# Window attention and two MLPs: scores of the float32 items folded to 128 columns, and a planner that knows when v lands

## The chip, the cores and the metric

One core of one Trainium2 chip. The metric is device time in microseconds of one execution, lower is better. PE is TensorE, DVE VectorE, ACT ScalarE, POOL GpSimd, SP the engine whose queue issues the loads.

## The reference

```python
# attention: B, H, S, D = 4, 8, 576, 64; window 128
scores = q @ k.T / sqrt(D) - slope[h] * abs(i - j)      # where 0 <= i - j < 128, else -1e9
attn = exp(scores - max(scores)); attn = attn / (sum(attn) + 1e-9)
x = (attn @ v)                                          # as 2304 x 512
# first MLP: 512 -> 2048 -> 512
h = x @ w_in; g = max(h, 0) + alpha * min(h, 0); x = g @ w_out
# second MLP: 512 -> 2048 -> 512
h = x @ w2_in; g = h / (1 + exp(-1.702 * h)); out = g @ w2_out
```

All inputs and the output are float32. Slopes are 2^-(h+1).

## The kernel before

The attention is cut into 64 items, one for each batch, head and unit. Unit 0 holds the queries 0 to 255 (32 items), unit 1 the rest. The first 24 items (`FP = 24`), all of unit 0, are computed in float32 at the start of the kernel and are called the float32 items; the other 40 are split into high and low parts and run later, beside the first MLP. Items are numbered n; two neighbouring items are two heads.

A unit 0 item has two chunks of 128 queries. The first attends to 128 keys, the second to 256: the 128 keys before it (of which a query sees those of an upper triangle) and its own 128 (a lower triangle). For each query exactly one of the two keys in the same column of these halves is inside the window. Steps of a float32 item, with the name that the planner gives them:

- raw: q, k and v are loaded by SP in two DMAs (L516 to L520), into five buffers in turn.
- s: scores on PE, one matmul a chunk, 128 and 256 columns (L568).
- bias: on DVE, scores plus bias with a running minimum, one custom instruction a chunk (L596), with a small instruction that reads the minimum out. The bias table relht has 256 columns a head, in bfloat16; outside the window it holds a large negative number.
- exp on ACT, an instruction a chunk (L612); add on POOL, sum plus 1e-9 (L627); recip (L622) and norm (L643, two scalings) on DVE.
- tr: on PE, transposes of 128 x 128 by an identity matrix, one for the first chunk and two for the second (L658); pt: ACT copies the 384 columns out of PSUM (L665).
- vz: POOL copies v beside zeros (L554), so that two heads share one output; x: on PE, attention times v (L715), two matmuls of 256 and 128 columns.
- xh on ACT and xl on DVE split the output of a pair of heads (L200, L205) for the MLP, which multiplies in three passes (high by high, high by low, low by high).

Weights of the first MLP come as 64-bit words and are decoded in 32 chunks: ld (SP), sc1 and sc2 (ACT, L245, L251), sh and ad (DVE, L255, L260), hi (ACT, L200), lo (DVE, L205). These are steps of the planner as well. The first MLP has steps h (L786, 12 matmuls), n (L800, ACT), g (L806, DVE), gh (ACT), gl (DVE) and o (L836, 12 matmuls). Step i of h needs weight chunk 2 * (i // 2), and g of step i - 2.

What sets the order: `emission()` runs a list planner over all these steps. PE's order is written out by hand: in each round scores of item n + 1, warm-up matmuls (`WARM`, only in the first seven rounds), v of item n - XLAG, transposes of item n - 1; after the rounds the h and o steps. The other engines take, among steps whose needs are met, the one that can start first and then the one with the earliest due time, worked out from a cost for each step (`COST`) and a delay for each engine (`DELAY`). `FIRST` gives the times at which the first five loads of q and k land; v is taken to be there with them. The list is issued in the order of planned start times, and `chain` fixes that order on each engine. Before the list stand memsets, the loads of the first five items and of the bias table (in four DMAs, for heads 0, 1, 2 to 3 and 4 to 7), and nine warm-up matmuls.

After the float32 items come 32 planned steps of the first MLP with the weight decoding beside them, from step 28 on with the split items; then the rest of the first MLP and the second, in an order of their own that the diff does not touch.

Of the kernel before, what the change touches and what calls it, by code (L numbers as in the profile page):

```python
# [39 lines left out]
PTF = {0: (0, 256, 0), 1: (256, 192, 128)}  # L40
# [28 lines left out]
EXTRA = {("g", SPLIT): 1.5}  # L69
# [4 lines left out]
def emission():  # L74
# [10 lines left out]
    for i in range(FP):  # L85
        ops |= {(k, i) for k in ("bias", "exp", "add", "recip", "norm", "vz", "pt")}
        ops |= {(k, i) for k in ("xh", "xl")[: 2 * (i % 2)]} | {("raw", i)}
# [4 lines left out]
    def needs(k, i):  # L92
        if k in ("s", "tr"):
# [3 lines left out]
            x=(("pt", i), ("vz", i), ("xl", i - 3)),  # L97
# [10 lines left out]
    deps = {z: [y for y in needs(*z) if y in ops] for z in ops}  # L108
    after = {z: [] for z in ops}
    for z in ops:  # L110
        for y in deps[z]:
            after[y].append((z, DELAY[COST[y[0]][0]] if COST[y[0]][0] != COST[z[0]][0] else 0))
# [18 lines left out]
    free, end, out = dict.fromkeys(ENGINES, 0.0), {}, []  # L131
# [3 lines left out]
    while any(wait.values()):  # L135
        best = None
        for e, l in wait.items():
            for z in l[: 1 if e == "PE" else 40]:
                if all(y in end for y in deps[z]):
                    t = max([free[e]] + [end[y] + (DELAY[COST[y[0]][0]] if COST[y[0]][0] != e else 0) for y in deps[z]])  # L140
# [22 lines left out]
def tile_window_attention__then__two_mlps(  # L163
# [265 lines left out]
    vzf = [first.tile([P, 2, P], F32, name=f"vzf{i}") for i in range(2)]  # L429
# [14 lines left out]
    def make_own():  # L444
        for t, n, below in ((own, P, False), (own2, D, True)):
            nc.gpsimd.memset(t, 1.0)
            nc.gpsimd.affine_select(
                out=t, in_=t, pattern=[[1 if below else -1, n]], compare_op=ALU.is_ge,
                fill=0.0, base=0, channel_multiplier=-1 if below else 1,
            )  # L450
# [97 lines left out]
    def a_split_v(n, b, u, h, U):  # L548
# [3 lines left out]
        if n < FP:  # L552
            d0 = (h % 2) * D
            nc.gpsimd.tensor_copy(vzs[n % 4][:, :, d0 : d0 + D], vr)  # L554
            return
# [5 lines left out]
    def a_qk(n, b, u, h, U):  # L561
        s = bank_of("s").rearrange("p (c k) -> p c k", k=256)
        places = []
        for i, (c0, rows, kk, keys) in enumerate(U["chunks"]):
            o = s[:rows, i, :]
            if n < FP:
# [4 lines left out]
                places.append(o[:, :keys])  # L571
# [7 lines left out]
        st["s", n] = places if n < FP else s  # L579

    @stage
    def a_bias(n, b, u, h, U):
        tt, s = work_of(n)
        places = st.pop(("s", n))
        m = len(U["chunks"])
        if n >= FP:
            x, places = places, []
            i0 = 1 - u
            nc.vector.copy_predicated(
                x[:, i0:m, :P], own.bitcast(U32).unsqueeze(1).to_broadcast([P, m - i0, P]), x[:, i0:m, P:]  # L590
            )
        for i, (c0, rows, kk, keys) in enumerate(U["chunks"]):
            off = kk - (c0 - P)
            if n >= FP:
                off = P if u == 0 and i == 0 else 0
            nc.vector.tensor_tensor_reduce(  # L596
                out=tt[:rows, i * 256 : i * 256 + keys] if n < FP else tt[:, i * P : (i + 1) * P],
                in0=places[i] if n < FP else x[:, i, :P],
                in1=relht[:rows, h, off : off + keys] if n < FP else relt[:, off : off + P],
# [4 lines left out]
                accum_out=s[:rows, i : i + 1],  # L604
# [3 lines left out]
    def a_exp(n, b, u, h, U):  # L608
        tt, s = work_of(n)
        for i, (c0, rows, kk, keys) in enumerate(U["chunks"]):  # L610
            t = tt[:rows, i * 256 : i * 256 + keys] if n < FP else tt[:, i * P : (i + 1) * P]
            nc.scalar.activation(  # L612
                t, t, AF.Exp, bias=s[:rows, i : i + 1], scale=-1.0, accum_out=s[:rows, 4 + i : 5 + i]
            )
# [14 lines left out]
    @stage  # L629
    def a_norm(n, b, u, h, U, eng):  # L630
        tt, s = work_of(n)
        if n >= FP:
            m = len(U["chunks"])
            t = tt[:, : m * P].rearrange("p (c k) -> p c k", k=P)
            nc.vector.tensor_tensor(t, t, s[:, 12 : 12 + m].unsqueeze(2).to_broadcast([P, m, P]), op=ALU.mult)
            return
        for i, (c0, rows, kk, keys) in enumerate(U["chunks"]):
            t = tt[:rows, i * 256 : i * 256 + keys]
            r = s[:rows, 12 + i : 13 + i]
            if eng == "act" or (eng == "mix" and i):  # L640
                nc.scalar.mul(t, t, r)
            else:
                nc.vector.tensor_scalar(t, t, r, None, op0=ALU.mult)  # L643

    @stage
    def a_trans(n, b, u, h, U):
        tt = work_of(n)[0]
        x = bank_of("pt")
        for i, (c0, rows, kk, keys) in enumerate(U["chunks"]):
            if n >= FP:  # L650
                keep(nc.tensor.transpose(x[:, i * P : (i + 1) * P], tt[:, i * P : (i + 1) * P], ident))  # L651
                continue
            for j in range(kk // P, (kk + keys) // P):
                col, nq, oc = PTF[j]
                dst = col + (c0 - U["q0"] - oc)

                src = tt[:, i * 256 + j * P - kk : i * 256 + j * P - kk + P]
                nc.tensor.transpose(x[:, dst : dst + P], src, ident)  # L658
# [3 lines left out]
    def a_pt_hi(n, b, u, h, U):  # L662
        x = st["t", n]
        if n < FP:
            nc.scalar.copy(pts[n % 3], x[:, :384])  # L665
        else:
            nc.scalar.copy(ar["th"][:, : U["nq"]], x[:, : U["nq"]])

# [36 lines left out]
    def a_av(n, b, u, h, U):  # L705
        if n < FP:
# [6 lines left out]
            pt, vz = pts[n % 3], vzs[n % 4]  # L713
# [459 lines left out]
    for t in vzs:  # L1173
        nc.gpsimd.memset(t, 0.0)
    for t in sts:
        nc.gpsimd.memset(t, 1.0)
# [6 lines left out]
    bias_load(0, 1)  # L1183
# [3 lines left out]
    bias_load(1, 1)  # L1187
    a_load(1, (1,))
    a_load(3, (0,))
    bias_load(2, 2)  # L1190
# [3 lines left out]
    bias_load(4, 4)  # L1194
    a_load(4, (1,))
    make_identity(nc, ident)
    make_own()
# [18 lines left out]
    def piece(name, fn):  # L1216
# [8 lines left out]
        norm=lambda n: a_norm(n, "dve"), vz=a_split_v, pt=a_pt_hi, xh=lambda n: a_xf(n, 0), xl=lambda n: a_xf(n, 1),  # L1225
        raw=a_load, ld=piece("load", w_load), sc1=w_scale_hi, sc2=piece("scale", w_scale_lo), sh=piece("shift", w_shift),
# [25 lines left out]
    def item_b(n):  # L1252
        o = n - 1 if n > FP else -1
        return (
            lambda: (n == FP + 2 and item_t(o), a_recip(n), a_split_v(n), a_load(n + 2), a_norm(n, "dve")),
# [18 lines left out]
    for k, i in emission():  # L1274
        if (k, i) == ("n", 0):
            joint()
        if k == "n" and i % 2:
# [277 lines left out]
```

## Time and profile before

| | us |
|---|---|
| median of the three runs shown | 873.68 |
| the runs | 873.65, 873.68, 881.98 |
| the profiled execution, its own time | 872.37 |
| its span, first to last instruction | 870.5 |
| PE busy in it | 862.5 (99%) |
| DVE, ACT, POOL busy | 695.5, 550.3, 186.1 |

The profile is of one execution. Times in a timeline are microseconds from the first instruction. A PE instruction counts as busy from its issue to a modelled end, so that a PE that is busy by the rows may still have waited; the distance from start to start tells it. The same distance is what an instruction costs on the other engines, since the end of one overlaps the beginning of the next.

### The profile page before, as it was taken

What the parts mean: (1) busy time and instruction counts of PE and PEld (TensorE: products, weight loads), DVE (VectorE), ACT (ScalarE), POOL (GpSimd) and SP (SyncE); (2) the same over time, 40 slices, a digit from 0 to 9 for tenths busy, and PEclk for the clock granted to TensorE, in tenths of its full rate; (3) what the DMA queues carried; (4) which work ended last, traced back from release to release, by engine and by line L of the source; (5) the groups of instructions that cost most, each with busy time, mean ns of one, the idle gap of its engine ahead of it and who ended that gap; (6) DMA issues with size and microseconds to landing.
All of it is one profiled execution on the core that took longest, in us unless ns stands there. A gap on an engine that the chain in (4) does not pass through costs nothing.

```text
span 870.5 us, 19438 instructions
## 1 busy us (share of the span) xinstructions
PE 862.5 (99%) x6804; PEld 835.7 (96%) x6804; DVE 695.5 (80%) x1763; ACT 550.3 (63%) x1397; POOL 186.1 (21%) x351
## 2 busy tenths in 40 slices
PE   9999999999999999999999999999999999999998
PEld 7899999999999999999988889999999999999998
DVE  6899886789899999998477777547474799988875
ACT  6999877677766776766355558656556764444433
POOL 4300003456656656655000000000000000000000
PEclk9999999999999999999999999999999999999999
DMA  5857742235244343351043344766678873634423
GB/s 156 218 158 230 249 138 95 78 98 178 78 125 152 91 127 115 90 172 29 25 146 98 98 142 147 235 222 230 233 250 293 286 249 112 178 125 134 146 61 98
DMA packets 74210, 132.29 MB, mean 152 GB/s; under 512 B 14336, under 2 KB 33792, under 8 KB 74112
## 3 DMA queue, kind: packets, MB, share of 16 engines
q1 hardware_dynamic: 74112, 131.05, 47.4%
q8 instruction: 54, 0.88, 0.4%
q14 instruction: 44, 0.36, 0.1%
HBM read 94.31 MB, written 36.70 MB: 151 GB/s over the span
## 4 chain that ended last, share of the span: by engine, by line
PE 61%; ACT 0%; DVE 0%; issue 0%; DVEq 0%; ACTq 0%
PE p L1092 19%; PE p L995 15%; PE h L786 9%; PE h L995 6%; PE p L836 5%; PE o L836 4%; PE x L727 1%; PE s L577 1%; PE pt L651 0%; PE s L578 0%; ACT oh L200 0%; DVE ob L1109 0%; ACT G L1004 0%; DVE se L1109 0%; DVE wd L1109 0%
## 5 line engine op out<-in xcount | busy, mean ns | idle before, releaser
L786 PE MATMUL h<-xh,wh 128*128 128x256 f32 (+1 forms) x512 | 149.2, 291 | 0.1
L786 PE MATMUL h<-xh,wl 128*128 128x256 f32 (+1 forms) x512 | 149.0, 291 | 0.0
L786 PE MATMUL h<-xl,wh 128*128 128x256 f32 (+1 forms) x512 | 149.0, 291 | 0.0
L1092 PE MATMUL p<-wl,oh 128*128 128x256 f32 x504 | 136.2, 276 | 0.0
L1092 PE MATMUL p<-wh,oh 128*128 128x256 f32 x504 | 135.0, 277 | 0.3 <-ACT oh L200 0.3
L1092 PE MATMUL p<-wh,ol 128*128 128x256 f32 x504 | 131.1, 276 | 0.0
L836 PE MATMUL o<-gh,wh 128*128 128x256 f32 x448 | 127.6, 285 | 0.0
L836 PE MATMUL o<-gl,wh 128*128 128x256 f32 x448 | 124.1, 277 | 0.8 <-DVE gl L205 0.8
L836 PE MATMUL o<-gh,wl 128*128 128x256 f32 x448 | 123.8, 276 | 0.0
L786 PEld LDWEIGHTS h<-xh,wh 128*128 128x128 f32 x512 | 96.1, 188 | 3.1 <-DVE g L806 0.3
L786 PEld LDWEIGHTS h<-xh,wl 128*128 128x128 f32 x512 | 96.1, 188 | 2.9
L786 PEld LDWEIGHTS h<-xl,wh 128*128 128x128 f32 x512 | 96.1, 188 | 2.7
L1123 POOL TENSOR_TENSOR ob<-wd,se 128x256 f32<-128x256 f32 x1 | 0.7, 746 | 448.2 <-ACT se L1121 448.2
L1092 PEld LDWEIGHTS p<-wl,oh 128*128 128x128 f32 x504 | 94.6, 188 | 0.0
L1092 PEld LDWEIGHTS p<-wh,oh 128*128 128x128 f32 x504 | 93.7, 188 | 0.5 <-ACT oh L200 0.5
L1092 PEld LDWEIGHTS p<-wh,ol 128*128 128x128 f32 x504 | 91.4, 188 | 0.0
L836 PEld LDWEIGHTS o<-gl,wh 128*128 128x128 f32 x448 | 84.3, 188 | 1.1 <-DVE gl L205 1.0
L836 PEld LDWEIGHTS o<-gh,wh 128*128 128x128 f32 x448 | 84.2, 188 | 0.1
L836 PEld LDWEIGHTS o<-gh,wl 128*128 128x128 f32 x448 | 84.1, 188 | 0.0
L800 ACT ACTIVATE n<-h 128x256 f32<-128x256 f32 (+1 forms) x128 | 52.2, 408 | 50.5 <-PE h L786 50.0
L812 ACT CAST gh<-g 128x256 fp32r<-128x256 f32 x112 | 45.3, 404 | 56.3 <-DVE g L806 56.2
L200 ACT CAST oh<-gs 128x1024 fp32r<-128x1024 f32 (+1 forms) x40 | 38.1, 964 | 62.9 <-issue 28.2
(190 smaller groups left out, 2459.2 us busy)
## 6 DMA issues: line engine op xcount, KB each, us to landing
g2d<-G SPq DMA_DIRECT2D x64, 288.0 KB, 3.5
ws<-in_w_in_dram SPq DMA_DIRECT2D x32, 512.0 KB, 3.8
ws<-in_w_out_dram SPq DMA_DIRECT2D x32, 512.0 KB, 4.4
gr<-g2d SPq DMA_DIRECT2D x32, 512.0 KB, 4.3
raw<-in_u_dram SPq DMA_DIRECT2D x32, 352.0 KB, 3.0
raw<-in_u_dram SPq DMA_DIRECT2D x32, 160.0 KB, 2.5
xr<-x2d SPq DMA_DIRECT2D x40, 128.0 KB, 2.6
wo2d<-wd SPq DMA_DIRECT2D x16, 256.0 KB, 2.6
```

The source lines that it names most:

```text
L200: return nc.scalar.copy(o, i)
L577: keep(nc.tensor.matmul(o[:, :n_], q, kh[:, ks : ks + n_], start=True, stop=False))
L727: keep(nc.tensor.matmul(x[:, oc : oc + nq], v, p[:, col : col + nq], start=(i == 0 and k == 0), stop=(i == len(js) - 1 and k == (j < 4)), ...
L786: keep(nc.tensor.matmul(ph, w[:, 0, c * P : (c + 1) * P], x[:, c, r : r + n], start=(c == 0 and i == 0), stop=(c == NC - 1 and i == 2),))
L800: nc.scalar.activation(n, ph, AF.Relu, scale=-1.0)
L812: nc.scalar.copy(gh, g)
L836: keep(nc.tensor.matmul(o, w[:, 1, c * P : (c + 1) * P], g, start=(first and (k == KM or c % 2 == 0) and i == 0), stop=(last and i == 2), ...
L995: tc.keep_in_program_order(nc.tensor.matmul(o, w[:, cc * P : (cc + 1) * P], x[:, h, cc, i, :], start=first and cc == 0 and k == 0, stop=la ...
L1092: mm = nc.tensor.matmul(o[:, m, :], g[:, a, m * P : (m + 1) * P], w, start=(p == 0 and m == 0 and i == 0), stop=(p == NF // 2 - 1 and i == 2),
L1123: nc.gpsimd.tensor_tensor(c11, p1_, p2_, op=ALU.add)
```

## The change

The float32 items are brought to the form of the later items of unit 0. DVE copies the own half of the second chunk's scores over the other half where a triangular mask `own` is set, then adds the bias on 128 columns for both chunks. For this the bias table is folded once: for each group of heads the larger of its two halves is kept, right before the bias of its first item (`HEADS`). Exponentials, scaling (now one instruction with the reciprocals spread over 128 columns each) and transposes (now two) work on 2 x 128 columns. After ACT's copy of 256 columns POOL separates the two triangles of the second chunk (own, then prev, in place); v's matmuls are as before.

The planner: new steps own and prev, new costs, v a known time for the first five items (`FIRST_V`), v matmuls a round later (`XLAG = 4`), six vz buffers instead of four, loads of weights due one round earlier and half a microsecond later in landing (`LATE`). A decoding step that it would place gives way to another step of that engine that is due sooner and can start before the decoding step would be nearly done (`DECODE`).

The start: masks are built before the identity matrix, some memsets go from POOL to DVE, and a small exponential is issued before the list.

```diff
-XLAG = 3
+XLAG = 4
+HEADS = {0: 1, 1: 1, 2: 2, 4: 4}
 ENGINES = dict(
-    PE=dict(s=0.66, tr=0.33, x=0.65, b=0.22, h=1.37, o=1.37),
-    DVE=dict(bias=0.6, recip=0.22, norm=0.5, xl=0.37, sh=0.4, ad=0.63, lo=0.63, g=0.42, gl=0.38),
-    ACT=dict(exp=0.98, pt=0.42, xh=0.31, sc1=0.6, sc2=0.6, hi=0.55, n=0.36, gh=0.34),
-    POOL=dict(vz=0.33, add=0.24),
+    PE=dict(s=0.66, tr=0.22, x=0.65, b=0.22, h=1.37, o=1.37),
+    DVE=dict(bias=0.78, recip=0.22, norm=0.37, xl=0.37, sh=0.4, ad=0.63, lo=0.63, g=0.42, gl=0.38),
+    ACT=dict(exp=0.81, pt=0.29, xh=0.31, sc1=0.6, sc2=0.6, hi=0.55, n=0.36, gh=0.34),
+    POOL=dict(vz=0.33, add=0.24, own=0.31, prev=0.31),
     SP=dict(raw=0.85, ld=2.3),
 )
-COST = {k: (e, c) for e, d in ENGINES.items() for k, c in d.items()}
+COST = {"v": ("SP", 0.0)} | {k: (e, c) for e, d in ENGINES.items() for k, c in d.items()}
+LATE = dict(ld=0.5)
+DECODE = ("sc1", "sc2", "sh", "ad", "hi", "lo")
+FIRST_V = (0.6, 1.8, 4.0, 5.2, 7.6)
-EXTRA = {("g", SPLIT): 1.5}
+EXTRA = {("g", SPLIT): 1.5} | {("bias", i): 0.14 * m for i, m in HEADS.items()}
...
-            x=(("pt", i), ("vz", i), ("xl", i - 3)),
+            x=(("prev", i), ("vz", i), ("xl", i - 3)), own=(("pt", i), ("x", i - 3)), prev=(("own", i),),
-            norm=(("recip", i),), pt=(("tr", i), ("x", i - 3)), vz=(("raw", i), ("x", i - 4)),
+            norm=(("recip", i),), pt=(("tr", i), ("x", i - 3)), vz=(("raw", i), ("v", i), ("x", i - 6)),
-            ld=(("ad", i - NST), ("s", 8 + 2 * i)), sc1=(("ld", i), ("lo", i - NWD)), sc2=(("ld", i),), sh=(("sc1", i),),
+            ld=(("ad", i - NST), ("s", 6 + 2 * i)), sc1=(("ld", i), ("lo", i - NWD)), sc2=(("ld", i),), sh=(("sc1", i),),
...
+        if z[0] in DECODE:
+            near = [(max([free[e]] + [end[y] + lag(y, x) for y in deps[x]]), x) for x in wait[e]
+                    if x[0] not in DECODE and due[x] < due[z] and all(y in end for y in deps[x])]
+            t, z = min([x for x in near if x[0] < t + cost(z) - 0.3], default=(t, z))
...
 def a_bias(n, b, u, h, U):
-        if n >= FP:
-            x, places = places, []
-            i0 = 1 - u
-            nc.vector.copy_predicated(
-                x[:, i0:m, :P], own.bitcast(U32).unsqueeze(1).to_broadcast([P, m - i0, P]), x[:, i0:m, P:]
-            )
+        i0 = 1 - u
+        nc.vector.copy_predicated(
+            x[:, i0:m, :P], own.bitcast(U32).unsqueeze(1).to_broadcast([P, m - i0, P]), x[:, i0:m, P:]
+        )
...
 def a_norm(n, b, u, h, U):
-        for i, (c0, rows, kk, keys) in enumerate(U["chunks"]):
-            t = tt[:rows, i * 256 : i * 256 + keys]
...
-                nc.vector.tensor_scalar(t, t, r, None, op0=ALU.mult)
+        t = tt[:, : m * P].rearrange("p (c k) -> p c k", k=P)
+        nc.vector.tensor_tensor(t, t, s[:, 12 : 12 + m].unsqueeze(2).to_broadcast([P, m, P]), op=ALU.mult)
...
 def a_pt_hi(n, b, u, h, U):
-            nc.scalar.copy(pts[n % 3], x[:, :384])
+            nc.scalar.copy(pts[n % 3][:, : 2 * P], x[:, : 2 * P])
...
+    def a_tri(o, t, below):
+        nc.gpsimd.affine_select(
+            out=o, in_=t, pattern=[[1 if below else -1, P]], compare_op=ALU.is_ge if below else ALU.is_gt,
+            fill=0.0, base=0, channel_multiplier=-1 if below else 1,
+        )
...
+    def a_pt_tri(n, b, u, h, U, below):
+        o, t = pts[n % 3][:, (1 + below) * P : (2 + below) * P], pts[n % 3][:, P : 2 * P]
+        a_tri(o, t, below)
...
+    make_own(own, P, False)
-    for t in vzs:
+    for t in vzs[:2]:
         nc.gpsimd.memset(t, 0.0)
+    make_identity(nc, ident)
+    make_own(own2, D, True)
     for t in sts:
-        nc.gpsimd.memset(t, 1.0)
+        nc.vector.memset(t, 1.0)
+    for t in vzs[2:]:
+        nc.vector.memset(t, 0.0)
+    nc.vector.memset(tb[:, :1], 0.0)
...
-    make_identity(nc, ident)
-    make_own()
+    nc.scalar.activation(tb[:, 1:2], tb[:, :1], AF.Exp)
...
     for k, i in emission():
+        if k == "bias" and i in HEADS:
+            t = relht[:, i : i + HEADS[i]]
+            nc.vector.tensor_tensor(t[:, :, :P], t[:, :, :P], t[:, :, P:], op=ALU.max)
```

## Rows read from the trace of the kernel before

**Rows 1.** Busy time of each engine in stretches: microseconds from and to, then each engine

```profile
core 0: us, PE busy (x) PEld busy (x) DVE busy (x) ACT busy (x) POOL busy (x), PEclk, DMA share, GB/s
11.40:44.00 32.60, 32.28 (x211) 29.43 (x210) 27.98 (x146) 29.39 (x109) 10.72 (x38) 1.00 0.74 197
44.00:52.10 8.10, 7.55 (x54) 6.70 (x52) 7.04 (x22) 7.67 (x21) 1.70 (x12) 1.00 0.31 92
52.10:80.00 27.90, 27.90 (x246) 27.90 (x247) 27.21 (x59) 27.06 (x59) 0.00 (x0) 1.00 0.66 211
...
5.60:52.10 46.50, 45.63 (x296) 40.17 (x294) 39.46 (x191) 41.40 (x145) 13.99 (x56) 1.00 0.66 178
```

**Rows 2.** Timeline of PE, one round of the float32 items: start, duration, instruction

```profile
18.51 0.49 PE L658 MATMUL pt<-ident,tt 128*128 128x128 f32 x3
18.83 0.82 PE L568 MATMUL s<-rawf 128*128 128x128 f32 x4
19.49 0.82 PE L715 MATMUL o<-ptf,vz 128*128 128x256 f32 x4
20.14 0.27 PE L658 MATMUL pt<-ident,tt 128*128 128x128 f32 x1
```

**Rows 3.** Timeline at the handover to the first MLP, PE and DVE

```profile
48.99 0.37 PE L786 MATMUL h<-xh,wh 128*128 128x256 f32 x1
...
50.94 0.69 DVE L205 TENSOR_TENSOR wl<-wd,wh 128x512 fp32r<-128x512 f32 x1 [0.24 <-ACT wh L200]
51.55 0.47 DVE L806 SCALAR_TENSOR_TENSOR g<-n,beta,h 128x256 f32<-128x256 f32 x1
...
52.08 0.38 PE L786 MATMUL h<-xh,wh 128*128 128x256 f32 x1
```

**Rows 4.** Who DVE waits for, 5.60 to 52.10: total, times, longest

```profile
DVE tt L596 <- PE s L568: 4.8, 5, 3.2
DVE st L622 <- POOL st L627: 1.3, 3, 0.5
DVE ttf L596 <- PE s L568: 0.4, 2, 0.2
```

**Rows 5.** Timeline of DVE, an item before, with the xl of a pair

```profile
19.69 0.29 DVE L596 CUSTOM_DVE_ANT_0 tt<-s,relht 128x128 f32<-128x128 f32 x1 [0.21 <-PE s L568]
...
20.25 0.16 DVE L622 RECIPROCAL st<-st 128x2 f32<-128x2 f32 x1
20.52 0.55 DVE L643 TENSOR_SCALAR ttf<-ttf,st 128x128 f32<-128x128 f32 x2
20.99 0.42 DVE L205 TENSOR_TENSOR xl<-o,xh 128x256 fp32r<-128x256 f32 x1
21.33 0.29 DVE L596 CUSTOM_DVE_ANT_0 tt<-s,relht 128x128 f32<-128x128 f32 x1
```

**Rows 6.** Timeline of DVE, item 24, which has the folded form before the change

```profile
125.36 0.29 DVE L589 COPY_PREDICATED s<-own,s 128x128 f32<-128x128 uint32 x1
...
126.11 0.08 DVE L596 DVE_READ_ACCUMULATOR2_ANT st<- 128x1 f32 x1
...
127.14 0.17 DVE L622 RECIPROCAL st<-st 128x2 f32<-128x2 f32 x1
127.34 0.42 DVE L635 TENSOR_TENSOR ts<-ts,st 128x256 f32<-128x256 f32 x1
127.68 0.69 DVE L205 TENSOR_TENSOR gl<-g,gh 128x256 fp32r<-128x256 f32 x1
...
135.88 0.42 DVE L205 TENSOR_TENSOR gl<-g,gh 128x256 fp32r<-128x256 f32 x1
```

**Rows 7.** POOL beside the split items: a timeline row, then groups (busy, mean ns)

```profile
127.48 0.61 POOL L205 TENSOR_TENSOR vp<-raw,vp 128x128 fp32r<-128x128 f32 x1 [0.95 <-ACT vp L557]
...
L676 POOL TENSOR_SCALAR_AFFINE_SELECT ptl<-tl 128x128 fp32r<-128x128 f32 x5 | 2.2, 436 | 1.4 <-DVE st L621 0.7 <-DVE tl L205 0.5
...
L676 POOL TENSOR_SCALAR_AFFINE_SELECT pth<-th 128x128 fp32r<-128x128 f32 x5 | 1.5, 302 | 6.3 <-ACT th L667 6.1
```

More of the change, by code (lines that the diff above doesn't have):

```diff
@@ L85, in emission @@
     for i in range(FP):
-        ops |= {(k, i) for k in ("bias", "exp", "add", "recip", "norm", "vz", "pt")}
+        ops |= {(k, i) for k in ("bias", "exp", "add", "recip", "norm", "vz", "pt", "own", "prev")}
         ops |= {(k, i) for k in ("xh", "xl")[: 2 * (i % 2)]} | {("raw", i)}
@@ L106, in needs, with lag @@
         )[k]
-    deps = {z: [y for y in needs(*z) if y in ops] for z in ops}
-    after = {z: [] for z in ops}
+    def lag(y, z):
+        e = COST[y[0]][0]
+        return DELAY[e] + LATE.get(y[0], 0) if e != COST[z[0]][0] else 0
+    known = {("v", i): t - DELAY["SP"] for i, t in enumerate(FIRST_V)}
+    deps = {z: [y for y in needs(*z) if y in ops or y in known] for z in ops}
+    after = {z: [] for z in (*ops, *known)}
     for z in ops:
         for y in deps[z]:
-            after[y].append((z, DELAY[COST[y[0]][0]] if COST[y[0]][0] != COST[z[0]][0] else 0))
+            after[y].append((z, lag(y, z)))
     for y, z in zip(seq, seq[1:]):
@@ L130, in emission @@
     wait = {e: sorted((z for z in ops if COST[z[0]][0] == e), key=lambda z: (place.get(z, 0), due[z], z)) for e in ENGINES}
-    free, end, out = dict.fromkeys(ENGINES, 0.0), {}, []
+    free, end, out = dict.fromkeys(ENGINES, 0.0), known, []
     for i, t in enumerate(FIRST):
@@ L139, in emission @@
                 if all(y in end for y in deps[z]):
[L140 removed]
+                    t = max([free[e]] + [end[y] + lag(y, z) for y in deps[z]])
                     if best is None or (round(t, 3), due[z], z) < best[0]:
@@ L428, in tile_window_attention__then__two_mlps @@
     rawfs = [first.tile([P, UCOLS[0]], F32, name=f"rawf{i}") for i in range(3)]
-    vzf = [first.tile([P, 2, P], F32, name=f"vzf{i}") for i in range(2)]
+    vzf = [first.tile([P, 2, P], F32, name=f"vzf{i}") for i in range(4)]
     at = ExitStack()
@@ L442, in tile_window_attention__then__two_mlps, with make_own @@
     own2 = ap_.tile([D, D], F32, name="own2")
-    def make_own():
-        for t, n, below in ((own, P, False), (own2, D, True)):
-            nc.gpsimd.memset(t, 1.0)
-            nc.gpsimd.affine_select(
-                out=t, in_=t, pattern=[[1 if below else -1, n]], compare_op=ALU.is_ge,
-                fill=0.0, base=0, channel_multiplier=-1 if below else 1,
-            )
+    def make_own(t, n, below):
+        nc.gpsimd.memset(t, 1.0)
+        nc.gpsimd.affine_select(
+            out=t, in_=t, pattern=[[1 if below else -1, n]], compare_op=ALU.is_ge,
+            fill=0.0, base=0, channel_multiplier=-1 if below else 1,
+        )
     def bank_of(kind):
@@ L603, in a_bias @@
                 op1=ALU.min,
-                accum_out=s[:rows, i : i + 1],
+                accum_out=s[:, i : i + 1],
             )
@@ L609, in a_exp @@
         tt, s = work_of(n)
[L610 to L614, printed above, removed]
+        for i in range(len(U["chunks"])):
+            t = tt[:, i * P : (i + 1) * P]
+            nc.scalar.activation(t, t, AF.Exp, bias=s[:, i : i + 1], scale=-1.0, accum_out=s[:, 4 + i : 5 + i])
     @stage
@@ L629, in a_norm @@
     @stage
-    def a_norm(n, b, u, h, U, eng):
+    def a_norm(n, b, u, h, U):
         tt, s = work_of(n)
[L632 to L637, printed above, removed]
-            t = tt[:rows, i * 256 : i * 256 + keys]
[L639 to L642, printed above, removed]
-                nc.vector.tensor_scalar(t, t, r, None, op0=ALU.mult)
+        m = len(U["chunks"])
+        t = tt[:, : m * P].rearrange("p (c k) -> p c k", k=P)
+        nc.vector.tensor_tensor(t, t, s[:, 12 : 12 + m].unsqueeze(2).to_broadcast([P, m, P]), op=ALU.mult)
     @stage
@@ L648, in a_trans @@
         x = bank_of("pt")
-        for i, (c0, rows, kk, keys) in enumerate(U["chunks"]):
+        for i in range(len(U["chunks"])):
+            t = nc.tensor.transpose(x[:, i * P : (i + 1) * P], tt[:, i * P : (i + 1) * P], ident)
             if n >= FP:
[L651 to L658, printed above, removed]
+                keep(t)
         st["t", n] = x
```

42 lines of the change are left out of this document (20 added, 22 removed).

## The prediction, made before the run

> **What bounds the kernel now.** I read the stretches first (busy time of each engine in five windows), then PE's timeline in the attention stage, then the handover to the first MLP, then who VectorE (DVE) waits for, and last the instructions of one item on DVE before and of one item that already runs in the new form. The granted clock is 1.00 in every stretch [rows 1], so nothing here turns on it. From 52.1 us on PE streams without a break (27.90 of 27.90 us) and its matmuls are not touched by the change; what the change can move is the moment at which that stream starts. So the question is when the third MLP matmul group starts, 52.08 us now.
>
> In the attention stage PE has a fixed round for each of the 24 items: three transposes 0.32 us (18.51 to 18.83), scores 0.66, attention times v 0.65, together 1.63 us [rows 2]. From 18.51 to the first MLP matmul at 48.99 it has 18 transpose groups, 16 of scores and 19 of v to do: 18 x 0.32 + 16 x 0.66 + 19 x 0.65 = 28.7 us in 30.5 us. So PE loses 1.8 us there to waiting, although its busy row shows next to nothing idle. The other engines are as full: in 11.4 to 44.0 us DVE is busy 27.98 and ACT 29.39 of 32.6 us, in 44.0 to 52.1 DVE 7.04 and ACT 7.67 of 8.1 us [rows 1].
>
> At the handover the one that comes last is DVE: the split of the third weight chunk (50.94, 0.69 us), then g of the first group (51.55, 0.47 us, so until 52.02), and 0.06 us later PE starts its third group [rows 3]. Everything DVE must do for the 24 items and for three weight chunks has to lie before that. I therefore add up DVE's time, not PE's.
>
> **The change, part by part.**
>
> *Two transposes instead of three.* A transpose follows the one before it after (0.49 - 0.27) / 2 = 0.11 us [rows 2]. PE's round becomes 1.52 us; over 24 items PE saves 2.6 us. Were PE the bound, this would be a gain in full.
>
> *The same items on DVE.* Before, one item takes 0.56 us from its first bias instruction to the reciprocal (19.69 to 20.25), 0.27 to the scaling, 0.47 for the two scalings, and every second item 0.34 for the low part xl [rows 5]. The new form is in this trace already, at item 24 (same unit, two chunks of 128 columns): copy-predicated and two reductions 125.36 to 126.11 = 0.75 us, reciprocal to scaling 0.20, one scaling over 256 columns 0.34 [rows 6]. So +0.19, -0.07 and -0.13: -0.01 us an item, -0.2 us over 24. DVE gains nothing from the fold; with xl it needs 1.46 us of PE's new 1.52 us round, so that the weight work (about 1.6 us a chunk on DVE) still has no room of its own.
>
> *Folding the bias table.* Four new DVE instructions, over 1, 1, 2 and 4 heads of 128 columns, each right in front of the bias of heads 0, 1, 2 and 4. Nearest rows: a tensor-tensor over 256 columns moves the next instruction by 0.34 us (20.99 to 21.33) [rows 5], one over 512 by 0.61 us (50.94 to 51.55) [rows 3]; by the same slope 0.20 over 128. Sum 0.20 + 0.20 + 0.34 + 0.61 = 1.35 us. The first lies where DVE waits 3.2 us for its first scores [rows 4], the second in the wait for the second scores; 0.95 us stay. They wait for the table's loads too; those of later heads land well before. Bounds: 0 (all in waits of the filling pipeline) to 1.35; I take 0.95.
>
> *What DVE stops waiting for.* From 5.60 to 52.10 us DVE is busy 39.46 of 46.50 us [rows 1]; of the 7.0 us idle, 4.8 + 0.4 - 3.2 = 2.0 us are waits for scores and 1.3 us waits for POOL's sum [rows 4]; the rest is short gaps and weight steps that wait for ACT. With PE's round 0.11 us shorter most waits for scores in the steady part go; in the filling part they stay, since warm-up matmuls set the pace there: 1.2 of 2.0. The scheduler that knows v's landing no longer puts item 1's copy of v ahead of item 0's sum, and one that looks past decoding delays fewer sums: half of the 1.3, 0.65. ACT exponentiates and copies 256 instead of 384 columns an item, so its weight steps come earlier: 0.45. Together 2.3 us, bounds 0 (each gap only moves) to 3.3 + 0.45.
>
> *Edits costed at nothing.* The table load stands at the front already, and ACT is idle until its first exponential; the new dummy one waits for a memset behind seven others on DVE, all in the 3.2 us before the first scores [rows 4]. POOL loses four memsets to DVE there. With v used one round later (XLAG 4, six v buffers) the pipeline drains later: behind the last transposes stand two more selects on POOL of 0.30 to 0.44 us [rows 7], 0.6 to 0.9 us on the last v matmul, and PE's MLP groups queue behind it in program order. PE then comes to its first group that much later after its last transpose, but the third group waits for DVE anyway; if that cover goes, it costs up to 0.9 us. Weight loads are issued one round earlier on SP's queue, between the item loads; DVE's clock is what they feed, and it has no room to use them sooner.
>
> *POOL.* It gets two selects an item: 2 x 0.30 (or 0.44) [rows 7]. It was busy 10.72 of 32.6 us [rows 1]; twenty items add 12.0 to 17.4 us, so it ends at 70% to 86%. It stays under PE's round, so I take no cost, but each sum can now stand behind a select.
>
> *A conflict of two engines.* The low part gl takes 0.69 us where POOL's subtraction of v starts just before it (127.48) and 0.42 us without one (135.88) [rows 6, 7]. The new scaling multiplies two tiles in SBUF, and POOL's new selects read SBUF: each meeting could cost 0.27 us. I take nothing in the sum, since the old scaling and POOL's copies already share these microseconds, and treat it as a rival. The Trainium skill (SBUF — State Buffer, section Who interferes with whom) has this as a rule: a VectorE instruction with two SBUF inputs and a GpSimd instruction that reads SBUF take one port in turns, and whichever starts second waits for the other to finish. By that rule, which the pair of rows bears out, the fold would be paid for on DVE.
>
> **The sum.** 2.3 + 0.2 - 0.95 = 1.5 us earlier start of the stream. The profiled execution took 872.37 us (870.5 span and 1.9 around it) and would take 870.9; the runs shown have their median 1.3 us above that, at 873.68, so the predicted median is 872.2.
>
> **Rivals.**
> 1. *PE is the bound after all.* Then the 2.6 us and the 1.8 us of waiting both go: 4.4 us, 869.3. For it: PE's round is longer than DVE's for an item. Against: DVE's last instruction releases the third group [rows 3], and its total does not fall.
> 2. *Nothing moves.* The gaps on DVE only change place and the table's folding eats what goes: 873.7, within 0.5. For it: the zero bound above, and 3.7 us of DVE's idle time are not waits that the change names.
> 3. *POOL and DVE get in each other's way* (slower). Place: the scaling of each item, and the sum behind POOL's selects. Price 0.27 us for each meeting; it decides from 1.5 / 0.27 = 6 of 24 items on. With 12 of them hit it costs 3.2 us: 873.68 - 1.5 + 3.2 = 875.4. For it: POOL busy over 70%. Against: the order on both engines is fixed and may keep them apart.
> 4. *The fold does not take hold* (the transposes stay at three, or PE's rounds keep 1.63 us): this is case 2 in time.
>
> **How the numbers follow.** Forecast (0.5 to 3 us gained, 870.7 to 873.2) 0.50; rival 1, 0.12; rivals 2 and 4, 0.20; rival 3, 0.18. The range runs from 869.6 (most of rival 1) to 875.6 (most of rival 3); the forecast alone would be 870.7 to 873.2. One per cent, about what a measurement of this kernel can tell from no change, is 8.7 us: twice the whole of rival 1, and four to five times rival 3. So no change within 1% has 0.97, slower 0.02 (for many meetings at POOL along with a late drain), faster 0.01.
>
> **What would show it.** Right: transposes in pairs and rounds near 1.52 us where no weight step stands; the bias of an item 0.75 us and its scaling 0.34 us on DVE; DVE's waits for scores near 0.8 us after the first; the third MLP group at 50.3 to 51.0 us, still released by DVE; everything behind it as before, only earlier. Wrong: the third group before 49.5 us, or released by PE's own last v matmul (rival 1, or a drain that counts); scalings of 0.6 us and more beside POOL's selects, or rounds over 1.63 us (rival 3). A change of more than 1 us between the third group and the end would mean that the order of later work moved too, which I take as unchanged.

## The result, and the profile after

The changed kernel takes 879.39 us (median of 22 runs, 875.96 to 887.2) against 873.66 us before (22 runs, 872.58 to 881.98): ratio 1.0055, 95% interval 1.0039 to 1.0072. It is 5.7 us slower, where 1.5 us less was forecast, and it lies above the range. The profiled execution of after took 887.2 us (span 885.2). From about 710 us on it ran at a pace that the other profiles show only near their end, so behind 140 us I read a second profile of the same kernel (878.2 us span).

First the busy time in the first two stretches of [rows 1], with two stretches more:

```profile
11.40:44.00 32.60, 29.87 (x172) 26.40 (x173) 25.77 (x135) 24.52 (x99) 21.34 (x74) 0.90 0.69 180
44.00:52.10 8.10, 7.45 (x47) 6.47 (x46) 7.37 (x33) 7.07 (x27) 5.98 (x19) 1.00 0.01 4
10.40:14.10 3.70, 0.07 (x1) 0.00 (x1) 0.71 (x3) 0.38 (x2) 1.45 (x6) 0.80 0.51 146
14.10:19.60 5.50, 5.47 (x19) 4.30 (x20) 3.71 (x20) 2.29 (x10) 2.19 (x9) 0.51 0.33 86
```

All engines but POOL are less busy up to 44 us, and PE does 172 instructions instead of 211, partly because it has fewer transposes, partly because it lost time: it stands from 10.40 to 14.10, and then the granted clock is 0.51 (the level of 1.2 GHz) until 19.60. Before, it was 1.00 throughout. The standstill, read from PE, DVE and POOL of after in turn (start, duration, instruction, idle time before it and what ended that):

```profile
14.13 0.66 PE L644 MATMUL pt<-ident,tt 128*128 128x128 f32 x2 [3.66 <-DVE tt L637]
```

```profile
13.28 0.17 DVE L625 RECIPROCAL st<-st 128x2 f32<-128x2 f32 x1 [3.29 <-POOL st L630]
13.55 0.42 DVE L637 TENSOR_TENSOR tt<-tt,st 128x256 f32<-128x256 f32 x1
```

```profile
8.00 0.22 POOL L630 TENSOR_SCALAR st<-st 128x2 f32<-128x2 f32 x1 [1.16 <-ACT tt L617]
12.43 0.29 POOL L565 COPY vzf<-raw 128x128 f32<-128x128 f32 x1 [4.22 <-DMA raw<-in_u_dram]
...
13.04 0.21 POOL L630 TENSOR_SCALAR st<-st 128x2 f32<-128x2 f32 x1
```

PE waits for item 1's scaling, DVE for item 1's sum, and POOL, which makes that sum, for a DMA. What stands in front of the sum is the copy of v of item **5** (12.43), whose loads SP issues at 8.65 and 9.22:

```profile
8.65 0.47 SPq L529 DMA_DIRECT2D raw<-in_u_dram  x1
9.22 0.54 SPq L531 DMA_DIRECT2D raw<-in_u_dram  x1
```

POOL's order in after is: copies of items 0 and 1, sum 0, copies of items 5 and 2, sum 1. Before, the copy of item 5 came behind the sum of item 4.

The waits of [rows 4] are in after, over the same stretch (total, times, longest):

```profile
DVE st L625 <- POOL st L630: 4.7, 2, 3.3
DVE s L596 <- PE s L578: 3.5, 4, 2.3
```

Waits for scores went from 5.2 to 3.5 us; without the first one (3.2 and 2.3 us), from 2.0 to 1.2 us, where the forecast wanted 0.8. The wait for POOL's sum, 1.3 before, became 4.7. The first MLP group starts at 53.80 instead of 48.99, and g ends at 56.50, before PE wants it, so that DVE no longer releases the third group, answering to [rows 3]:

```profile
53.80 0.36 PE L785 MATMUL h<-xh,wh 128*128 128x256 f32 x1
...
56.71 0.28 PE L785 MATMUL h<-xh,wh 128*128 128x256 f32 x1
```

```profile
55.42 0.69 DVE L217 TENSOR_TENSOR wl<-wd,wh 128x512 fp32r<-128x512 f32 x1
56.02 0.48 DVE L805 SCALAR_TENSOR_TENSOR g<-n,beta,h 128x256 f32<-128x256 f32 x1
```

So the third group comes 56.71 - 52.08 = 4.6 us late. The steady round and DVE's item look as forecast, answering to [rows 2, 5]:

```profile
26.13 0.38 PE L644 MATMUL pt<-ident,tt 128*128 128x128 f32 x2
...
27.66 0.38 PE L644 MATMUL pt<-ident,ttf 128*128 128x128 f32 x2
```

```profile
25.70 0.29 DVE L596 COPY_PREDICATED s<-own,s 128x128 f32<-128x128 uint32 x1
...
26.45 0.42 DVE L217 TENSOR_TENSOR xl<-o,xh 128x256 fp32r<-128x256 f32 x1
26.79 0.16 DVE L625 RECIPROCAL st<-st 128x2 f32<-128x2 f32 x1
27.05 0.43 DVE L637 TENSOR_TENSOR ttf<-ttf,st 128x256 f32<-128x256 f32 x1
27.39 0.29 DVE L596 COPY_PREDICATED s<-own,s 128x128 f32<-128x128 uint32 x1
```

A second loss lies where nothing was changed. Item 24's first v matmul starts at 137.75 us before and at 145.58 after (145.52 in the second profile): 7.8 us late, 3.2 more than the third group. PE is busy all the time and the clock is granted in full, but fewer matmuls fit. The window 60 to 120 us, before, then after:

```profile
60.00:120.00 60.00, 60.00 (x532) 60.00 (x531) 57.03 (x122) 55.63 (x121) 0.00 (x0) 1.00 0.74 235
```

```profile
60.00:120.00 60.00, 60.00 (x512) 60.00 (x511) 53.93 (x113) 52.86 (x111) 0.00 (x0) 1.00 0.64 209
```

60 us over 532 matmuls are 113 ns each, over 512 they are 117. I call this the pace; from start to start, away from the few longer steps, it is 113 or 118 ns. In before the stream runs at 113 ns to 124.6 us, at 118 to about 134 us, and at 113 again; in after it runs at 118 from 53.9 to about 142 us. Of the 3.2 us, 0.5 is a longer wait for gl (1.33 instead of 0.82 us); the rest fits some 640 matmuls by 4.5 ns, an estimate from these rows of 2.9 us. Behind item 24 nothing is lost in the second profile: 878.2 - 145.52 = 732.7 us there, 870.5 - 137.75 = 732.8 us before. The profiled execution of 887.2 us has the slow pace once more in its last stretch. 720 to 840 us, after, then the second profile of it:

```profile
720.00:840.00 120.00, 120.00 (x1022) 120.00 (x1021) 103.48 (x202) 51.26 (x82) 0.00 (x0) 1.00 0.45 136
```

```profile
720.00:840.00 120.00, 120.00 (x1061) 120.00 (x1060) 108.16 (x210) 52.31 (x84) 0.00 (x0) 1.00 0.46 137
```

### The profile page after: what moved, and what is told of

It reads as the page before. It is cut to its first block, busy times and chain, and to the rows that moved or that the text cites. A ratio compares the mean times of both kernels' runs of the same rounds, so it can differ in the third digit from the quotient of the medians.

```text
span 885.2 us, 19424 instructions
## 1 busy us (share of the span) xinstructions
PE 872.4 (99%) x6780; PEld 844.2 (95%) x6780; DVE 700.1 (79%) x1775; ACT 548.4 (62%) x1398; POOL 201.2 (23%) x394
## 4 chain that ended last, share of the span: by engine, by line
PE 60%; DMA 1%; ACT 0%; DVE 0%; issue 0%; ACTq 0%; DVEq 0%
PE p L1091 19%; PE p L994 14%; PE h L785 9%; PE h L994 6%; PE p L835 5%; PE o L835 4%; PE x L726 1%; PE s L586 1%; DMA g2d<-G 1%; PE pt L644 0%; PE s L587 0%; ACT oh L212 0%; DVE ob L1108 0%; ACT wh L212 0%; ACT G L1003 0%
## 5 line engine op out<-in xcount | busy, mean ns | idle before, releaser
L1091 PE MATMUL p<-wl,oh 128*128 128x256 f32 x504 | 138.6, 281 | 0.0
L1091 PE MATMUL p<-wh,oh 128*128 128x256 f32 x504 | 137.4, 281 | 0.5 <-ACT oh L212 0.5
L1091 PE MATMUL p<-wh,ol 128*128 128x256 f32 x504 | 133.4, 281 | 0.4 <-DVE ol L217 0.4
L835 PE MATMUL o<-gl,wh 128*128 128x256 f32 x448 | 124.6, 278 | 1.3 <-DVE gl L217 1.3
```

The costliest lines, as they stand in the source:

```text
L835: keep(nc.tensor.matmul(o, w[:, 1, c * P : (c + 1) * P], g, start=(first and (k == KM or c % 2 == 0) and i == 0), stop=(last and i == 2), ...
L1091: mm = nc.tensor.matmul(o[:, m, :], g[:, a, m * P : (m + 1) * P], w, start=(p == 0 and m == 0 and i == 0), stop=(p == NF // 2 - 1 and i == 2),
```

## The experiments

Three theories came out of this. **Q**: the copy of v of item 5 stands too early in POOL's queue. **C**: the low clock after the standstill is a cost of its own. **P**: the pace of the unbroken stream has two values, and which one is taken depends on how the stream begins. Two rivals stand in the expectations: **F**, the fold itself costs the time, and **L**, the slower pace comes from what else runs beside it. Unless a line says otherwise, ratios are against the kernel before, timed alongside.

**1. The changed kernel again**, beside the next three.

> The changed kernel once more, for a second profile beside its variants. In its first profile PE stands still for 3.66 us at 10.5 to 14.1 us: the scaling of item 1 waits for POOL's sum, and POOL stands at the copy of item 5's v, whose load lands at 12.4 us. Every theory expects the same stall here, a first MLP group near 53.8 us and about 879 us.

Measured: 880.05 us, before 875.49 (31 runs), ratio 1.0049 [1.0019, 1.0079]. The stall is there again (3.51 us), and so is the pace of 118 ns up to item 24.

**2. Item 5's copy held back** by what its wait was before, x of item i - 4; the rest stays.

```diff
-vz=(("raw", i), ("v", i), ("x", i - 6))
+vz=(("raw", i), ("v", i), ("x", i - 4))
```

> The changed kernel with one condition of the planner put back: a copy of v waits for the v matmul four items before it, as before the change, not six. Theory Q (the queue: item 5's copy stands in front of item 1's sum on POOL and waits for a load that SP issues behind 15 others) expects the stall of 3.66 us at PE's second pair of transposes and the low clock after it to go, the third MLP group near 51 us, and 871.5 to 873 us. Rival F (the fold itself costs: selects on POOL, the new scaling and the late drain) expects only the stall's 3.7 us back and 875 us or more.

Measured: 874.99 us, ratio 0.9994 [0.9960, 1.0027]; seven of ten runs between 874.04 and 875.41. That is above what Q expected and at the edge of what F did. The stall is gone, but the first MLP group starts only at 52.50. PE now waits for the items' loads (PE's waits, 5 to 52 us):

```profile
PE s L578 <- DMA raw<-in_u_dram: 1.8, 2, 1.5
PE s L578 <- DMA rawf<-in_u_dram: 1.7, 2, 1.4
```

Item i's load waits for item i - 5's copy. With XLAG 4, x comes a round later, so a copy that waits for x of i - 4 comes later too, and so does the load. So with XLAG 4 the six buffers have a use, and the fault to look for is the planner's guess of the load.

**3. The planner told that SP is busy** with the first loads: its SP queue starts at 5.0 instead of 0.

```diff
-free, end, out = dict.fromkeys(ENGINES, 0.0), known, []
+free, end, out = dict.fromkeys(ENGINES, 0.0) | dict(SP=5.0), known, []
```

> The changed kernel, with the planner told that SP is busy with the first loads until 5.0 us of its own time; six v buffers and everything else stay. Theory Q expects the stall gone as in the variant with four, 871.5 to 873 us, and item 5's copy of v behind the sums of items 1 to 3. Rival F expects 875 us or more. If only the distance of four items helped, this one would stay at 879 us.

Measured: 875.51 us, ratio 1.0000 [0.9964, 1.0036]; five of ten runs between 872.78 and 874.76; Q expected 871.5 to 873. POOL takes the sum of item 1 at 8.97, and the copy of item 5 at 13.00, behind the sum of item 3 (12.72) and without waiting:

```profile
8.97 0.21 POOL L630 TENSOR_SCALAR st<-st 128x2 f32<-128x2 f32 x1 [0.52 <-ACT tt L617]
...
12.72 0.21 POOL L630 TENSOR_SCALAR st<-st 128x2 f32<-128x2 f32 x1
13.00 0.29 POOL L565 COPY vzf<-raw 128x128 f32<-128x128 f32 x1
```

The clock in 14.10 to 19.60 is 1.00, the first MLP group starts at 48.07, and the third at 50.90, 1.2 us before [rows 3]:

```profile
50.90 0.31 PE L785 MATMUL h<-xh,wh 128*128 128x256 f32 x1
51.05 0.28 PE L785 MATMUL h<-xl,wh 128*128 128x256 f32 x1
```

Q is shown: one number in the planner moves the third group from 56.71 to 50.90, 5.8 us, and the median from 880.05 to 875.51 on the same chip. The profile of one execution is less exact than these digits: experiments 6, 7 and 12 have the same program up to that point and reach it at 52.03, 52.52 and 51.84, in part because PE waits 0.7 to 0.9 us for loads in them. So what the order costs, the low clock included, lies between 4.2 and 5.8 us. Against before, nothing is left in the median of the 1.2 us. The step from 50.90 to 51.05 is 0.15 us instead of 0.11, and from there the stream runs at the slow pace:

```profile
60.00:120.00 60.00, 60.00 (x512) 60.00 (x511) 53.43 (x112) 52.58 (x110) 0.00 (x0) 1.00 0.68 208
```

**4. PE kept busy through the wait** with 18 warm-up matmuls at that place; POOL's order stays as in after.

```diff
-WARM = (9, 3, 3, 2, 1, 1, 1)
+WARM = (9, 3, 3, 2, 18, 1, 1)
```

> The changed kernel with 18 instead of 1 warm-up matmuls in the round in which PE stands still: PE computes through the wait, the wait itself stays. Theory C (part of the loss is the clock, which is granted at half for about 5 us after the stall) expects PE's matmul groups of 1.49 us between 14.6 and 19 us to be 0.82 us as elsewhere and 2 to 3 us less than the changed kernel, 876 to 877.5 us. If the stall alone counts, nothing changes: 879 us.

Measured: 877.87 us (0.4 above the range that C expected), ratio 1.0018 [0.9981, 1.0056], 2.2 us less than after on the same chip (880.05). The transposes still come at 14.00, but the scores behind them take 0.82 instead of 1.49 us:

```profile
14.10:19.60 5.50, 5.45 (x34) 4.41 (x35) 4.98 (x27) 4.11 (x17) 4.11 (x14) 1.00 0.44 120
```

```profile
14.00 0.41 PE L644 MATMUL pt<-ident,tt 128*128 128x128 f32 x2 [0.52 <-DVE tt L637]
14.24 0.82 PE L578 MATMUL s<-rawf 128*128 128x128 f32 x4
```

The first MLP group starts at 51.39 instead of 53.73. C is shown, at 2.3 us; the standstill itself then costs what is left of the way to experiment 3, 51.39 - 48.07 = 3.3 us, or 1.7 to 2.4 us if the first group is taken from the profiles of experiments 6, 7 and 12 (49.21, 49.70, 49.02).

**5. The kernel before, with six v buffers and nothing else** of the change.

```diff
-vz=(("raw", i), ("x", i - 4))
+vz=(("raw", i), ("x", i - 6))
-vzf = [first.tile([P, 2, P], F32, name=f"vzf{i}") for i in range(2)]
+vzf = [first.tile([P, 2, P], F32, name=f"vzf{i}") for i in range(4)]
-nc.gpsimd.tensor_copy(vzs[n % 4][:, :, d0 : d0 + D], vr)
+nc.gpsimd.tensor_copy(vzs[n % 6][:, :, d0 : d0 + D], vr)
```

> The kernel before the change with one edit of it: six v buffers, and the planner lets a copy of v go as soon as the v matmul six items before it is done. The planner then puts item 5's copy in front of item 1's sum on POOL. Theory Q (the queue) expects the same stall as in the changed kernel, 3 to 4 us of PE around 10 to 14 us and the lower clock after it, and 4 to 6 us more than the kernel before. Rival F (the stall needs the fold, whose selects also stand on POOL) expects no stall and no change.

Measured: 878.39 us against 873.83 (27 runs), ratio 1.0056 [1.0033, 1.0079]: as much as the changed kernel loses, without the fold. F is out as the cause of the stall. POOL waits as in after, and PE's second group of transposes comes at 13.35 after 2.96 us without work:

```profile
12.05 0.29 POOL L554 COPY vzf<-raw 128x128 f32<-128x128 f32 x1 [3.57 <-DMA raw<-in_u_dram]
12.42 0.21 POOL L627 TENSOR_SCALAR st<-st 128x2 f32<-128x2 f32 x1
```

**6 and 7. The stream broken** by an additional float32 matmul of 128 columns ahead of a group, on top of experiment 3: once (third group), then four times (third, fifth, seventh, ninth). Its output is overwritten by the group. Each takes about 0.3 us. The diff is that of one break; with four, the condition is k == 0 and f in (1, 2, 3, 4).

```diff
+if (k, f) == (0, 1):
+    keep(nc.tensor.matmul(ph[:, :P], hi[:, 0, :P].bitcast(F32), xh[:, 0, r : r + P].bitcast(F32), start=True, stop=True))
```

> The changed kernel with SP's queue told to the planner, and one extra float32 matmul of 128 columns in front of the first MLP's third group (its result is overwritten). In the profile without it all matmuls of the first MLP from 51 to 126 us follow each other after 118 ns, where the kernel before has 113 ns from 52 to 124 us. Theory P (the pace is one of two, taken when PE's stream starts anew and kept until it is interrupted) expects the extra matmul to start the stream anew, most likely at 113 ns: item 24's scores 2.5 to 3 us earlier and 870.5 to 872 us. Rival L (the slower pace comes from what else runs in those microseconds) expects 118 ns again and 0.2 us more.

> The same with an extra matmul in front of four groups of the first MLP (third, fifth, seventh, ninth), 0.2 to 0.3 us each. Theory P expects a pace of 113 ns behind at least one of them, kept from there on, and 871 to 873 us. Rival L expects 118 ns throughout and 1 us more than without.

Measured: once 875.35 us (872.76 to 876.9, one 881.16), ratio 1.0013 [0.9992, 1.0035], 3.4 us above what P expected; four times 873.93, ratio 0.9993 [0.9981, 1.0005], all ten runs between 873.65 and 874.36, 0.9 above. Both profiles show the pace of 113 ns, as P had it. Behind the last break of the second, 311 matmuls in 35 us, 112.5 ns each:

```profile
85.00:120.00 35.00, 35.00 (x311) 35.00 (x310) 31.77 (x68) 31.53 (x65) 0.00 (x0) 1.00 0.67 216
```

Both streams were at 113 ns ahead of their first break too, so they show only that a break need not be followed by the slow pace. A break that ends the slow pace is in the profile of experiment 11: 12 matmuls take 1.42 us ahead of its third break (63.69 to 65.11) and 1.36 us behind it (69.49 to 70.85). Its first two breaks left the pace slow. With four breaks the scatter over 3 to 4 us goes; one break leaves it, which fits a stream that can take either pace again.

**8. The fold alone**: after, with the planner as it was before (no knowledge of v's landing, no look ahead, loads and copies at their old distances), but XLAG 4.

```diff
-known = {("v", i): t - DELAY["SP"] for i, t in enumerate(FIRST_V)}
+known = {}
-LATE = dict(ld=0.5)
+LATE = {}
-DECODE = ("sc1", "sc2", "sh", "ad", "hi", "lo")
+DECODE = ()
-vz=(("raw", i), ("v", i), ("x", i - 6))
+vz=(("raw", i), ("v", i), ("x", i - 4))
-ld=(("ad", i - NST), ("s", 6 + 2 * i))
+ld=(("ad", i - NST), ("s", 8 + 2 * i))
```

> The changed kernel without the planner's new knowledge: copies of v at a distance of four items, no landing times for v, no looking past decoding, weight loads as before the change. What stays is the fold, its two steps on POOL, the later v matmuls and the new start. Theory Q expects no stall of 3.7 us and 873 to 875 us. Rival F expects 875 us or more, with PE's rounds over 1.63 us.

Measured: 878.26 us (874.61 to 883.2), ratio 1.0046 [1.0025, 1.0067]. By the time F was right and Q wrong; F's sign, rounds over 1.63 us, is not there (undisturbed rounds take 1.53). The profile is without the stall and at the pace of 113 ns. The first MLP group starts at 51.78; as in experiment 2, PE waits for loads:

```profile
PE s L578 <- DMA rawf<-in_u_dram: 1.6, 1, 1.6
...
PE s L578 <- DMA raw<-in_u_dram: 0.6, 1, 0.6
```

The fold with the old planner isn't worth having; which of the edits taken back counts most was not separated. How much of the 4.4 us in the medians is the pace of the runs that weren't profiled stays open.

**9 and 10. After and before with the same four breaks**, so that both run at one pace.

> The changed kernel as it is, with four extra float32 matmuls in front of groups 3, 5, 7 and 9 of the first MLP. Theory P (the pace of the MLP's matmuls, 113 or 118 ns, is kept until the stream is interrupted) expects the pace of 118 ns to end behind one of them: 3 us less and 1 us for the four matmuls, so 877 to 878 us where the changed kernel has 879 to 880, with the stall and the low clock still there. If the pace were not part of the loss, it would be 1 us slower than the changed kernel.

> The kernel before the change with the same four extra matmuls. Its runs fall into two groups, 872.7 to 874.1 and 875.3 to 876.6 us. Theory P expects them in one, at 873.5 to 874.5 us, since the second group would be runs in the slower pace. If the groups have another cause, they stay, each 1 us later.

Measured: after 878.47 us (877.24 to 879.15, one 882.87; P expected 877 to 878), ratio 1.0051 [1.0028, 1.0074]; before 874.33 (873.8 to 875.23), ratio 1.0004 [0.9993, 1.0015]. Both profiles count 532 matmuls in 60 to 120 us. At equal pace the change costs 878.47 - 874.33 = 4.1 us.

**11. Everything but the fold**: three transposes, XLAG 3, the old costs and the old start, with the new planner, six buffers, the SP start of 5.0 and the four breaks.

> Three transposes and the old scaling, but all of the planner's new knowledge (v's landing, six v buffers, looking past decoding, earlier weight loads), SP's queue told to it, and the four extra matmuls. Beside the folded kernel with the same (873.9 us) it gives what the fold is worth once the queue is in order. The forecast's sum over DVE expects little: 0 to 1.5 us more than the folded one, 874 to 875.5 us. If PE were the bound, 2.6 us more or above, 876.5 us and up.

Measured: 874.95 us, ratio 1.0018 [1.0000, 1.0036], against 873.93 in experiment 7, which has the fold besides: the fold, with the XLAG, the costs and the start that go with it, is worth about 1.0 us. The two ran on different chips; against before on its own chip, one is 1.4 us slower and the other 0.1, and the intervals of the ratios overlap. So it is a small gain of uncertain size.

**12. The best of these**: experiment 3 with three short breaks, 32 columns, ahead of the third, fifth and ninth group.

```diff
+if k == 0 and f in (1, 2, 4):
+    keep(nc.tensor.matmul(ph[:, :32], hi[:, 0, :P].bitcast(F32), xh[:, 0, r : r + 32].bitcast(F32), start=True, stop=True))
```

> A candidate: the changed kernel with SP's queue told to the planner and three extra float32 matmuls of 32 columns (groups 3, 5 and 9 of the first MLP), about 0.2 us each. Theories Q and P together expect no stall at the start, 113 ns in the first MLP and 872 to 873.5 us, in one group of runs; a kernel without a gain from the fold would come to 873.5 to 875 us.

Measured: 873.35 us (12 runs, 872.3 to 874.07), ratio 0.9996 [0.9986, 1.0005]. It is 6.0 us below the 879.39 of the changed kernel (on another chip), and not to be told from the kernel before.

## Why the prediction was wrong

**The step that failed: "Edits costed at nothing".** There the six v buffers were looked at only for the late drain at the end of the stage. What they do at its start, where they let the planner put copies earlier in POOL's queue, was not worked out and so put at nothing, although [rows 4] already had DVE waiting for POOL's sum. Experiment 5 shows that this one edit in the kernel before costs 4.6 us in the medians, and experiment 3 that a planner with a later start of SP's queue takes it back. Related and wrong as well: "the scheduler that knows v's landing no longer puts item 1's copy of v ahead of item 0's sum". In after item 1's copy (6.54 us) still stands there, and item 5's stands ahead of item 1's sum. The planner knows the landing of items 0 to 4; for item 5 it reckons with an SP queue that is empty at 0, while the trace has it issuing first loads until after 8 us. In the queue as it is built, a copy waits for its DMA, a sum that was ready at 9.14 us waits behind it, and DVE and PE wait for the sum.

The drain at the end of the stage, which that step did name, is larger than its 0.6 to 0.9 us and is no longer covered. From the last transposes to the first MLP group PE takes 2.95 us in experiment 3 (2.95 in after too), where before it took 48.99 - 47.13 = 1.86. Before, then PE and POOL of experiment 3:

```profile
47.13 0.49 PE L658 MATMUL pt<-ident,ttf 128*128 128x128 f32 x3
```

```profile
45.12 0.41 PE L644 MATMUL pt<-ident,ttf 128*128 128x128 f32 x2
...
47.39 0.92 PE L714 MATMUL o<-ptf,vzf 128*128 128x256 f32 x4 [0.24 <-POOL ptf L658]
48.07 0.36 PE L785 MATMUL h<-xh,wh 128*128 128x256 f32 x1
```

```profile
44.32 1.86 POOL L658 TENSOR_SCALAR_AFFINE_SELECT pt<-pt 128x128 f32<-128x128 f32 x4
46.14 1.20 POOL L658 TENSOR_SCALAR_AFFINE_SELECT ptf<-ptf 128x128 f32<-128x128 f32 x2
```

PE's last v matmuls wait for the last of POOL's selects.

**"The granted clock is 1.00 in every stretch, so nothing here turns on it."** True of before only. A standstill of 3.66 us was followed by 5.5 us at 0.51; experiment 4 puts a price of 2.3 us on that. The Trainium skill (TensorE: Matmul & The Clock Gate, section HAM oscillation — how this bites in real kernels) has it that a PE which waits long enough for data between bursts starts the next one at the low clock. The trace agrees, 0.51 behind the wait.

**"Everything behind it as before, only earlier."** Wrong by 3.2 us between the third group and item 24, and this was the sign that the prediction named for a moved order; the order hadn't moved. It was the pace. Before's own trace had both values ahead of the forecast, 113 ns to 124.6 us and 118 from there to about 134, and I didn't look at distances in a stream that had no gap in it.

**What adds up.** Order put right (experiment 3), the third group comes 1.2 us earlier than before. The queue and the clock put it 56.71 - 50.90 = 5.8 us later than that: 4.6 us net in the profile, 4.1 us in the medians at equal pace (experiments 9 and 10). The first two figures carry the scatter of single profiles named at experiment 3. The medians without breaks differ by 5.7 us. I put the other 1.6 us to the pace: of after's 22 runs 20 took 877.48 us or more, while before's fell into two groups, in the last set 21 of 31 runs at 872.4 to 873.8 us and 10 at 875.2 to 876.4. That a run in the upper group has the slow pace is inferred, since only profiled executions show it; that the groups vanish with the breaks (874.33 us, all ten within 1.5) speaks for it.

**The terms of the sum** held better than the sum. *Gain at the third group*: forecast 1.5 us ("50.3 to 51.0 us"); with the order put right it came at 50.90, a gain of 1.2, in one profile, and at 51.84 to 52.52 in three others, against 52.08 and 52.80 in the two of before (experiment 10 is the second). So some gain is likely, but 1.5 us is not shown. *DVE's waits*: forecast 2.3 us less; in experiment 3 waits for scores after the first are 0.2 us (2.0 before) and there are none for POOL's sum (1.3 before), so this term was right in kind. *PE's round*: forecast 1.52, measured 27.66 - 26.13 = 1.53 us. *DVE's item*: bias forecast 0.75, measured 0.75 (25.70 to 26.45); reciprocal to scaling 0.20, measured 0.26; scaling 0.34, measured 0.34. *Folding the table*: forecast 1.35 us, of these 0.95 exposed. The four instructions, by columns, took 0.22, 0.23, 0.29 and 0.51 us, 1.25 in all. The third moved the next instruction by 0.20 us (8.96 to 9.16), not 0.34, and DVE waited 0.27 us for scores behind the fourth, so less than 0.95 was exposed. Three of the groups:

```profile
L1283 DVE TENSOR_TENSOR relht<-relht 128x512 bf16<-128x512 bf16 x1 | 0.5, 512 | 0.0
L1283 DVE TENSOR_TENSOR relht<-relht 128x256 bf16<-128x256 bf16 x1 | 0.3, 286 | 0.0
L1283 DVE TENSOR_TENSOR relht<-relht 128x128 bf16<-128x128 bf16 x1 | 0.2, 221 | 0.0
```

*The fold's worth over all*: about 1 us (experiments 7 and 11), not the 2.6 us that PE saves in transposes. That DVE alone sets the end, as the prediction said against rival 1, does not follow. In before PE stood still until g was done; in experiment 3 g ends at 50.77, and PE steps into the third group at 50.90, 0.11 us behind the matmul before it, as within the stream. Both come to that point together, and PE has given back 1.1 us of its saving in the drain.

```profile
50.30 0.47 DVE L805 SCALAR_TENSOR_TENSOR g<-n,beta,h 128x256 f32<-128x256 f32 x1
```


**The rivals.** Rival 1 (869.3 us) fell: no run with the order put right came near it. Rival 2, nothing moves, is the median of experiment 3, though for another reason: a gain at the third group and a slower stream behind it. Rival 3 had the right sign and the wrong place. POOL did hold the stage up, by the order of its queue and not by a port. The scalings, each with two inputs in SBUF beside POOL's selects, are in after (count, busy, mean ns):

```profile
L637 DVE TENSOR_TENSOR tt<-tt,st 128x256 f32<-128x256 f32 x16 | 6.8, 425 | 1.7
L637 DVE TENSOR_TENSOR ttf<-ttf,st 128x256 f32<-128x256 f32 x8 | 3.6, 452 | 0.8
```

24 scalings take 10.4 us, against 10.2 at the 0.425 us of most: 0.2 us in all (0.5 in experiment 3), where the rival needed 3.2. It is not that they don't meet: 16 of the 24 overlap a select. Two of these took 0.51 and 0.55 us; for the rest POOL paid, whose selects take 0.29 us alone and, but for two, 0.36 to 0.58 where they began inside a scaling. The rule cited in the prediction from the Trainium skill (SBUF — State Buffer, section Who interferes with whom) agrees with this, since most selects started second; the prediction had put its price on DVE. Most of the stage hides it. At the end it is not hidden: the last six selects of experiment 3 run without a break from 44.32 to 47.34, 0.50 us each, while DVE decodes weights, and PE waits for them. What that costs at the third group no run separates.

**The chances.** No change within 1% had 0.97, and 0.55% slower lies within; but the range ended at 875.6, because no case in it had a standstill at the stage's start. The rival on the slower side was built from a resource that would be fuller (POOL at 70 to 86%; it was 65%, 21.34 of 32.6 us), when what mattered was which of POOL's instructions stands in front of which.

## What to carry to other kernels

Where an edit relaxes a constraint of a planner (more buffers, an earlier allowed start), write down the first ten instructions of every in-order queue before and after, and ask of each one that waits for a DMA when that DMA is really issued: a planner that starts a queue empty when the program has filled it will put a wait ahead of work that is ready. A standstill early in a kernel can be paid twice, in the wait and at the low clock behind it. When two kernels differ by a few us in a stretch where PE never stops, count the matmuls in equal windows before looking for a cause in the order.

## What the runs showed that I had not expected

An unbroken stream of 128x256 float32r matmuls ran at one of two paces, 113 or 118 ns from start to start, at a granted clock of 1.00 in both. In every profile a value once taken was kept until the stream next stopped or another kind of instruction broke it: 53.9 to 142 us in after, 52 to 124.6 in before. The weight loads alongside take 187 to 188 ns at the fast pace, and every third one 192 at the slow. Why one value or the other is taken at a break isn't settled: in experiment 11 two breaks left the slow pace and the third ended it, a step of 0.15 us at the third group came ahead of the slow one in experiment 3, and a break put there ended in the fast one in the profiles of experiments 6 and 7. Over a last stretch of some 160 us it is worth 885.2 - 878.2 = 7.0 us between two executions of one kernel, more than the change itself.
